# Another order for the units of a pipelined attention round, on one core

## The chip, the core and the metric

The kernel runs on one core of a Trainium2 chip. The metric is the device time of one execution in microseconds (us). Of the kernel before there are three runs: 536.33, 537.93 and 538.74 us, median 537.93. Differences of about 0.5% (2.7 us) are what a measurement of this kernel can tell from no change.

## The reference

Three blocks follow each other. The first is block-causal attention on q, k, v of shape (4, 8, 576, 64), the second a dense layer pair with a bent activation, the third a soft mixture of 8 experts.

```python
scores = scale * np.matmul(q, k.transpose(0, 1, 3, 2))       # masked by blocks of 64
attn = softmax(scores); attn_out = np.matmul(attn, v)
x = attn_out as (2304, 512)
h = x @ w_in                                                  # 512 -> 2048
g = np.where(h >= 1, h, np.where(h <= -1, 0.0, (h + 1) ** 2 / 4))
x2 = g @ w_out
logits = x2 @ phi; slots, expert layers w1 and w2, and the weighted sum back to the tokens
```

## The kernel before, in words

**Engines.** TensorE (PE) multiplies, VectorE (DVE), ScalarE (ACT) and GpSimd (POOL) compute, SyncE (SP) issues all loads in one queue. Each engine works its own list strictly in order, so a list's head that waits holds everything behind it.

**Attention in pairs.** The 4 x 8 heads are worked in 16 pairs of two heads (class `Pair`, numbered 0 to 15, four to a batch; in a tile's name the batch is left out, so `sc_31` is the pair 3 of its batch, part 1). A pair goes through these units; the digit behind a unit's name is its part:

- `lk`, `lq`, `lv`: loads of k, q, v by SP (L60, L73, L74). `kh`, `kl`, `qh`, `ql`: k and q split into a rounded part (ACT; L254, L89) and a rest (POOL L83, DVE L95). After `ql` SP copies a piece of q into a doubled tile `QD` (L99).
- `sc0` to `sc4`: scores on PE (L113, L120), each into one of **two** large PSUM tiles; `mk` adds the mask. `mx` takes row maxima on DVE (L144, L146), `ex` the exponentials on ACT (L151), which frees the score tile for the score part two places later. `rs` sums and inverts on DVE (L157, L158), `no` normalises in place on POOL (L163).
- `pt0` to `pt6`: transposes of the probabilities on PE (L171), each into one of **three** small PSUM tiles of the pool `ptr` (L1131); `pc0` to `pc6` copy them out, `pc1` and `pc3` on DVE (L256), the others on ACT (L254).
- `pa`, `pb`: probabilities times v on PE (L189, L194). `pb` writes its output (`ps..o`) into a `ptr` tile too. `xh`, `xl` take the outputs away: for the first 1024 tokens `xh` is a cast on ACT (L217) and `xl` a subtraction on DVE (L223); for the later ones (pair 8 on, and the end of pairs 4 to 7) `xh` is a copy on DVE (L215) and `xl` does nothing.

**Early work of the second block.** Eleven units of `h = x @ w_in` are worked inside attention (dict `EARLY`, L234). The letters m, x, y, z are four parts of three matmuls on PE (L535) that sum into one `ptr` tile, so that this tile is held for a round and more; `a` is an activation on ACT (L556), `o` two instructions on DVE (L569, L570), the last of which frees the tile. The weights for it come as 64-bit words: `w0` loads a tile `raw` (SP L448), `w1` is one multiplication on ACT (L457) and four bit operations on DVE (L463 to L466), `w2` three operations on POOL (L258, L481, L482).

**What sets the order.** The string `PLAN` (L227) is one round, written out by hand or by a search: `4pt1` means part 1 of `pt` for the pair that started four rounds ago. The function `attention` (L248) unrolls 22 rounds and leaves out what has no pair (L284 to L287). Each engine's list is what the units add to it, one after another; nothing is reordered later. Waits are put in by the framework from who reads and writes what. Once attention is over, `Moe.run` follows with its own order, which is not touched.

```python
plan = [(it - int(u[0]), u[1:]) for it in range(n + 6) for u in PLAN.split()]
```

Of the kernel before, what the change touches and what calls it, by code (L numbers as in the profile page):

```python
# [224 lines left out]


PLAN = """  # L227
6xh1 2ho0 2lq 6xh0 4pt1 4mx0 6xl0 4no4 3sc2 3mx3 3mk2 2kh 4pt2 4ex0 1hy0
4rs1 2kl 4no1 4pt3 4pt5 1hz0 4no0 4pc1 3sc4 3mx2 2w1 6xl1 4pc0 4pt4 5pc6
2w2 3sc1 3ex3 3mk1 4pc2 1w0 5pa 3ex2 4pc5 3rs0 3mx4 3no3 2qh 4pc4 3mx1  # L230
5pb 0lk 2ql 3ex4 3sc0 4pc3 3lv 3mk0 3rs2 2sc3 3no2 2mk3 3pt0 1ha0 0hm0
4pt6 3ex1 0hx0
"""
EARLY = {(9, 0): (0, 0), (10, 0): (0, 1), (11, 0): (0, 2), (12, 0): (0, 3), (13, 0): (1, 0), (14, 0): (0, 4),  # L234
         (15, 0): (1, 1), (16, 0): (0, 5), (17, 0): (1, 2), (18, 0): (0, 6), (19, 0): (1, 3)}
# [980 lines left out]
```

## Time and profile before

| | us |
|---|---|
| median of three runs | 537.93 |
| the profiled execution's own time | 535.42 |
| its span, first to last instruction | 533.6 |
| PE busy | 506.3 (95%) |
| DVE busy | 337.5 (63%) |
| ACT busy | 322.2 (60%) |
| POOL busy | 199.4 (37%) |

The median lies 2.51 us above the profiled execution, and that one 1.82 us above its span. Attention takes the first 206 us of the span, the part from there on belongs to the second and third block. The busy shares above are means over all of it, while the three other engines are far busier in attention than later. A round shows in the trace as the stretch from the start of one pair's `pa` (PE, L189) to the start of the next one's.

### The profile page before, as it was taken

The page shows a single profiled execution, that of the slowest core. Times are in us where ns is not written, and L with a number is a line of the kernel's source. Part 1 is how long each engine was busy: PE and PEld are TensorE (multiplying, and loading weights), DVE is VectorE, ACT ScalarE, POOL GpSimd, SP SyncE. Part 2 cuts the span into 40 slices and gives each one's busy share as a digit, 9 for nine tenths or more (in the row PEclk, how much of TensorE's full clock was granted, in tenths as well). Part 3 has the DMA queues.
Part 4 walks back from the last instruction along what each step waited for, and adds up shares of the span by engine and source line. Part 5 has one row for each costly group of instructions (what it writes and reads, how often), then busy time and mean ns, then how long its engine had stood idle before and what let it go on. Part 6 is the DMA issues. An engine that isn't in the chain of part 4 may idle for free.

```text
span 533.6 us, 11818 instructions
## 1 busy us (share of the span) xinstructions
PE 506.3 (95%) x4538; PEld 382.0 (72%) x4538; DVE 337.5 (63%) x678; ACT 322.2 (60%) x732; POOL 199.4 (37%) x259
## 2 busy tenths in 40 slices
PE   6899999999999999999898999899999999989994
PEld 5688787777777777787666887788767888643463
DVE  7779888788887755888998546824454443531242
ACT  5799998776666644676867888634334545231131
POOL 4889987776665421555542213400001000010000
PEclk9799999999999999999999999999999999999997
DMA  5443453323211136312157874412166496799998
GB/s 177 120 135 114 138 147 85 112 73 112 73 51 50 28 107 211 146 40 80 39 166 217 299 240 166 160 59 79 51 254 226 146 383 208 276 330 390 409 413 313
DMA packets 42711, 91.01 MB, mean 171 GB/s; under 512 B 8736, under 2 KB 18080, under 8 KB 42656
## 3 DMA queue, kind: packets, MB, share of 16 engines
q1 hardware_dynamic: 42656, 90.26, 49.5%
q8 instruction: 36, 0.59, 0.4%
q14 instruction: 19, 0.16, 0.1%
HBM read 74.51 MB, written 14.68 MB: 167 GB/s over the span
## 4 chain that ended last, share of the span: by engine, by line
PE 75%; DVE 8%; ACT 7%; DMA 3%; issue 3%; POOL 2%; SPq 0%; DVEq 0%; ACTq 0%; POOLq 0%
PE h L535 30%; PE sc L120 6%; PE gn L592 5%; PE om L189 4%; PE lt L604 3%; PE s L642 3%; PE eh L998 3%; PE acc L1025 3%; PE ps_1p L171 2%; PE sc L113 2%; PE ps_2p L171 2%; PE ps_3p L171 2%; PE ps_0p L171 2%; ACT pr L151 2%; DMA raw<-in_w_out_dram 2%
## 5 line engine op out<-in xcount | busy, mean ns | idle before, releaser
L535 PE MATMUL h<-xh,w 128*128 128x512 f32 (+1 forms) x384 | 115.6, 369 | 0.0
L535 PE MATMUL h<-xt,w 128*128 128x512 f32 x384 | 98.2, 403 | 0.7 <-DVE g L570 0.2
L163 POOL TENSOR_SCALAR pr<-pr,sm 128x512 f32<-128x512 f32 (+2 forms) x144 | 86.0, 616 | 27.6 <-DVE sm L158 19.8
L151 ACT ACTIVATE pr<-sc,nm 128x512 f32<-128x512 f32 (+2 forms) x144 | 78.9, 561 | 14.6 <-DVE nm L146 8.1
L569 DVE SCALAR_TENSOR_TENSOR g<-g 128x512 f32<-128x512 f32 (+1 forms) x52 | 38.5, 740 | 66.9 <-ACT g L556 66.9
L535 PEld LDWEIGHTS h<-xt,w 128*128 128x128 f32 x384 | 68.3, 188 | 16.4 <-DVE g L570 1.8
L535 PEld LDWEIGHTS h<-xh,w 128*128 128x128 f32 x384 | 69.1, 189 | 13.8 <-issue 3.8
L535 PE MATMUL h<-xl,w 128*128 128x512 f32 (+1 forms) x192 | 68.2, 355 | 0.3 <-POOL xl L409 0.3
L570 DVE TENSOR_TENSOR g<-h,g 128x512 f32<-128x512 f32 (+1 forms) x80 | 50.8, 636 | 14.8 <-ACT g L561 12.8
L146 DVE TENSOR_REDUCE nm<-sc 128x2 f32<-128x1024 f32 (+1 forms) x64 | 51.9, 819 | 10.7 <-PE sc L126 9.6
L556 ACT ACTIVATE g<-h,half 128x512 f32<-128x512 f32 (+1 forms) x52 | 32.4, 623 | 43.3 <-PE h L535 43.0
L673 POOL TENSOR_TENSOR cn<-cn,cm 128x128 f32<-128x128 f32 (+1 forms) x5 | 1.9, 379 | 140.7 <-DVE cm L672 140.7
L120 PE MATMUL sc<-K,Q 64*128 64x512 f32 (+3 forms) x384 | 47.2, 360 | 3.4 <-ACT pr L151 2.9
L254 ACT COPY gn<-gn 128x1024 f32<-128x1024 f32 x35 | 35.3, 1009 | 16.0 <-PE gn L592 15.8
L535 PEld LDWEIGHTS h<-xl,w 128*128 128x128 f32 x192 | 36.4, 189 | 4.5 <-POOL xl L409 0.7
L120 PEld LDWEIGHTS sc<-K,Q 64*128 64x128 f32 x384 | 29.9, 194 | 13.3 <-ACT pr L151 4.7
L474 POOL TENSOR_TENSOR wab<-wab 128x512 f32<-128x512 f32 x16 | 22.0, 1373 | 40.8 <-DVE wab L466 30.7
L481 POOL TENSOR_TENSOR wab<-wab,w 128x256 f32<-128x256 f32 (+1 forms) x23 | 22.7, 985 | 38.9 <-ACT w L254 20.4
L592 PE MATMUL gn<-ident,g 128*128 128x128 f32 x280 | 36.5, 273 | 0.1
L592 PEld LDWEIGHTS gn<-ident,g 128*128 128x128 f32 x280 | 31.9, 140 | 5.3 <-issue 2.5
L464 DVE SCALAR_TENSOR_TENSOR wab<-wab 128x512 uint32<-128x512 uint32 (+1 forms) x39 | 28.5, 730 | 9.9 <-ACT wab L457 6.9
L558 ACT ACTIVATE g<-h,half 128x512 f32<-128x512 f32 x28 | 19.2, 687 | 22.7 <-PE h L535 20.3
(222 smaller groups left out, 896.5 us busy)
## 6 DMA issues: line engine op xcount, KB each, us to landing
ew<-in_w_dram SPq DMA_DIRECT2D x32, 512.0 KB, 5.9
raw<-in_w_in_dram SPq DMA_DIRECT2D x16, 512.0 KB, 5.1
raw<-in_w_out_dram SPq DMA_DIRECT2D x16, 512.0 KB, 4.3
ew<-in_w2a_dram SPq DMA_DIRECT2D x16, 510.0 KB, 8.9
ew<-in_w2b_dram SPq DMA_DIRECT2D x16, 344.0 KB, 6.8
kn<-in_k_dram SPq DMA_DIRECT2D x16, 288.0 KB, 4.4
qn<-in_q_dram SPq DMA_DIRECT2D x16, 288.0 KB, 3.9
vn<-in_v_dram SPq DMA_DIRECT2D x16, 256.0 KB, 3.0
```

The costliest lines, as they stand in the source:

```text
L120: nc.tensor.matmul(sc[:, h, 0:n], self.Q[r, qa, 128 * i:128 * i + 128], self.K[r, ka, 0:n], start=(k == 0), stop=False)
L146: nc.vector.tensor_reduce(out=self.negm[:, 2 * i:2 * i + 2], in_=self.scs[i][:, :, 0:128 * (i + 1)], axis=AX.X, op=ALU.max, negate=True)
L151: self.nc.scalar.activation(pr, sc, AF.Exp, bias=self.negm[:, b:b + 1], accum_out=self.acc[:, b, 0:1])
L163: self.nc.gpsimd.tensor_scalar(out=pr, in0=pr, scalar1=self.sums[:, b:b + 1], scalar2=1.0, op0=ALU.mult, op1=ALU.mult)
L171: nc.tensor.transpose(ps[:, u * P:(u + 1) * P], self.pr[b][:, kc * P:(kc + 1) * P], e.ident)
L254: nc.scalar.copy(dst, src)
L464: v.scalar_tensor_tensor(out=Au, in0=Au, scalar=3, in1=Bu, op0=ALU.logical_shift_left, op1=ALU.bitwise_or)
L535: nc.tensor.matmul(ph[:, 0:n], w[:, wi, kk], self.x(b, kk, xi)[:, 0:n], start=(kk + m == 0), stop=(kk + m == 5))
L556: nc.scalar.activation(g, ph, AF.Relu, bias=e.half[:, 0:1], scale=0.5)
L569: nc.vector.scalar_tensor_tensor(out=g, in0=g, scalar=1.0, in1=g, op0=ALU.min, op1=ALU.mult)
L570: nc.vector.tensor_tensor(out=g, in0=ph, in1=g, op=ALU.max)
L592: nc.tensor.transpose(ps[:, j, i * P:(i + 1) * P], self.gt(b, f)[:, o:o + P], e.ident)
```

## The change

Only the string `PLAN` is replaced. It holds the same units as before, each with the digit that says how many rounds behind it is; most digits grow by one, because the new string is cut at another point of the cycle (it begins just before `pb`, where the old one began just after `hx`). No instruction is added or removed: each engine has as many rows as before.

```diff
 PLAN = """
-6xh1 2ho0 2lq 6xh0 4pt1 4mx0 6xl0 4no4 3sc2 3mx3 3mk2 2kh 4pt2 4ex0 1hy0
...
+4mk1 3qh 6pb 6pa 4mx1 5pc5 2ha0 5pc4 6xh0 3w2 4sc0 2w0 3ql 4ex4 4no3
...
 """
```

Laid over each other as cycles, the two orders differ in these ways. On PE `pb` stands ahead of `pa`, `pt0` moves from behind `sc3` to behind `hy`, and `sc4` moves ahead of `pt5` and `hz`. On ACT the run `kh`, `ex0`, `w1`, `pc0`, `pc6`, `ex3`, `pc2`, `ex2`, `pc5`, `qh`, `pc4`, `ex4`, `a`, `ex1`, `xh1`, `xh0` becomes `kh`, `ex0`, `pc6`, `w1`, `ex3`, `pc2`, `ex2`, `pc0`, `qh`, `pc5`, `a`, `pc4`, `xh0`, `ex4`, `ex1`, `xh1`. On DVE `pc3` moves from behind `ql` to behind `mx2`, and the copies of x are taken apart: the one of `pb`'s output comes first, the ones of `pa`'s output after `mx0`. On SP the loads of q come a round earlier; those of v come later, one round ahead of their `pb` and no longer more than that, and `w0` later too, in the round of its `w1`.

DVE's list in the round in which pair 9 passes `pa` and `pb` (`ps_1o` is `pb`'s output, `om_1` that of `pa`, `nm` are row maxima, `g` and `h` belong to the early unit). Before:

```order
L146 TENSOR_REDUCE nm_3_2056<-sc_31_2118 128x2
L95 SCALAR_TENSOR_TENSOR Q_0_2159<-qn_0_2039,Q_0_2159 128x576
L256 COPY PT_2_2093<-ps_2p_2078 128x512
L157 TENSOR_REDUCE sm_3_2057<-ac_197 128x1
L158 RECIPROCAL sm_3_2057<-sm_3_2057 128x1
L215 COPY xw_148<-om_1_2132 128x128
L215 COPY xw_150<-om_1_2132 128x192
L569 SCALAR_TENSOR_TENSOR g_0_2204<-g_0_2204 128x512
L570 TENSOR_TENSOR g_0_2204<-h_0_2024,g_0_2204 128x512
L215 COPY xw_148<-ps_1o 128x256
L146 TENSOR_REDUCE nm_3_2056<-sc_30_2174 128x2
```

The same stretch of DVE's list now:

```order
L146 TENSOR_REDUCE nm_3_2058<-sc_31_2125 128x2
L215 COPY xw_148<-ps_1o 128x256
L95 SCALAR_TENSOR_TENSOR Q_0_2135<-qn_0_1908,Q_0_2135 128x576
L157 TENSOR_REDUCE sm_3_2059<-ac_197 128x1
L158 RECIPROCAL sm_3_2059<-sm_3_2059 128x1
L569 SCALAR_TENSOR_TENSOR g_0_2163<-g_0_2163 128x512
L570 TENSOR_TENSOR g_0_2163<-h_0_2021,g_0_2163 128x512
L146 TENSOR_REDUCE nm_3_2058<-sc_30_2170 128x2
L215 COPY xw_148<-om_1_2142 128x128
L215 COPY xw_150<-om_1_2142 128x192
```

Between `mx1` (first row) and `mx0` (the `sc_30` row) stood nine instructions and now stand six: `pc3` (the `PT` row) and the two copies from `om_1` are gone from there.

PE's list after the scores `sc3` of the same round (`ps_3p` are transposes `pt0` and `pt1`, `ps_2p` is `pt6`, `h_4` the early unit's parts m and x). Before:

```order
L171 MATMUL ps_3p_2199<-ident,pr_187 128x128
L171 MATMUL ps_3p_2199<-ident,pr_188 128x128
L171 MATMUL ps_3p_2199<-ident,pr_189 128x128
L171 MATMUL ps_3p_2199<-ident,pr_190 128x128
L535 MATMUL h_4_2206<-xt_140,w_1568 128x512 x3
L171 MATMUL ps_2p_2210<-ident,pr_176 128x128
L535 MATMUL h_4_2206<-xt_141,w_1568 128x512 x3
L171 MATMUL ps_3p_2224<-ident,pr_187 128x128
L171 MATMUL ps_3p_2224<-ident,pr_188 128x128
L171 MATMUL ps_3p_2224<-ident,pr_189 128x128
L171 MATMUL ps_3p_2224<-ident,pr_190 128x128
L120 MATMUL sc_02_2231<-K_0_2061,Q_0_2159 128x384 x6
```

The same stretch of PE's list now:

```order
L535 MATMUL h_4_2203<-xt_140,w_1619 128x512 x3
L171 MATMUL ps_2p_2209<-ident,pr_176 128x128
L171 MATMUL ps_3p_2211<-ident,pr_187 128x128
L171 MATMUL ps_3p_2211<-ident,pr_188 128x128
L171 MATMUL ps_3p_2211<-ident,pr_189 128x128
L171 MATMUL ps_3p_2211<-ident,pr_190 128x128
L535 MATMUL h_4_2203<-xt_141,w_1619 128x512 x3
L120 MATMUL sc_02_2230<-K_0_2037,Q_0_2135 128x384 x6
```

`pt0` has left this stretch and `pt1` stands one place earlier, between the two parts of the early unit.

SP's queue at the start (`kn`, `qn` loads of k and q, numbered by pair; `raw` the first weights). Before:

```order
L61 DMA kn_0_205<-in_k_dram 128x576
L61 DMA kn_1_207<-in_k_dram 128x576
L61 DMA qn_0_209<-in_q_dram 128x576
L448 DMA raw_214<-in_w_in_dram 128x1024
L61 DMA kn_2_218<-in_k_dram 128x576
L99 DMA QD_165<-Q_0_216 64x2x64 x2
L61 DMA qn_1_232<-in_q_dram 128x576
```

SP's queue at the start now:

```order
L61 DMA kn_0_205<-in_k_dram 128x576
L61 DMA kn_1_207<-in_k_dram 128x576
L61 DMA qn_0_209<-in_q_dram 128x576
L61 DMA kn_2_213<-in_k_dram 128x576
L61 DMA qn_1_216<-in_q_dram 128x576
L448 DMA raw_220<-in_w_in_dram 128x1024
L99 DMA QD_165<-Q_0_218 64x2x64 x2
```

The first weights have gone from the fourth place to the sixth, behind `kn_2` and `qn_1`.

## Rows read from the trace of the kernel before

**Rows 1.** Windows by round: length, busy of PE, PEld, DVE, ACT, POOL, PEclk, DMA.

```profile
60.80:70.25 9.45, 9.45 (x109) 7.70 (x111) 8.54 (x22) 9.35 (x30) 8.86 (x13) 1.00 0.48 142
70.25:82.48 12.23, 12.23 (x122) 9.85 (x123) 9.67 (x23) 10.29 (x31) 10.14 (x16) 1.00 0.42 123
...
120.25:133.62 13.37, 12.67 (x122) 9.74 (x120) 10.90 (x23) 9.35 (x29) 8.73 (x14) 1.00 0.38 112
...
186.26:196.33 10.07, 9.58 (x92) 7.38 (x93) 5.75 (x14) 4.88 (x16) 3.21 (x7) 1.00 0.43 140
196.33:202.96 6.63, 6.21 (x59) 4.31 (x61) 2.17 (x5) 1.44 (x3) 0.00 (x0) 1.00 0.40 127
```

**Rows 2.** Chain that ended last, 119 to 134.5 us: start, length, what.

```profile
120.92 1.18 DVE Q L95
122.11 0.60 DVE PT L256
...
122.97 0.45 DVE xw L215 x2
123.42 1.03 DVE g L569
...
124.48 0.70 DVE g L570
...
127.05 0.48 ACT PT L254
...
127.58 0.66 PE ps_2p L171 x4
```

**Rows 3.** PE's timeline, same round: start, length, instruction, [idle before <-who].

```profile
127.58 0.66 PE L171 MATMUL ps_2p<-ident,pr 128*128 128x128 f32 x4 [0.58 <-ACT PT L254]
```

**Rows 4.** Chain that ended last, PE in the round from 70.25 us.

```profile
70.25 1.66 PE om L189 x16
...
73.68 0.78 PE sc L120 x6
...
75.09 0.69 PE h L535 x3
```

**Rows 5.** ACT's timeline in a round without early work, from 51.33 us.

```profile
54.75 0.67 ACT L254 CAST K<-kn 128x576 fp32r<-128x576 f32 x1
...
56.98 0.72 ACT L151 ACTIVATE pr<-sc,nm 128x512 f32<-128x512 f32 x1
```

**Rows 6.** Chain that ended last, the start.

```profile
8.45 2.58 ACT pr L151 x8
...
15.63 1.90 PE ps_0p L171 x8
```

**Rows 7.** ACT's timeline at the start.

```profile
7.79 0.43 ACT L457 ACTIVATE wab<-raw 128x256 f32<-128x256 f32 x1 [1.47 <-DMA raw<-in_w_in_dram]
```

**Rows 8.** Windows at the start, columns as in rows 1.

```profile
3.00:4.00 1.00, 1.00 (x12) 1.00 (x11) 0.87 (x8) 0.00 (x0) 0.00 (x0) 1.00 1.04 396
...
12.00:18.00 6.00, 5.01 (x28) 3.95 (x30) 4.09 (x10) 4.75 (x16) 6.00 (x9) 0.50 0.35 73
...
19.00:25.00 6.00, 4.31 (x44) 3.73 (x42) 5.50 (x14) 5.59 (x16) 4.24 (x6) 1.00 0.38 142
...
29.00:32.00 3.00, 3.00 (x30) 2.83 (x28) 2.68 (x8) 2.30 (x7) 1.55 (x4) 1.00 0.33 126
```

**Rows 9.** Chain that ended last, the end of attention and what follows.

```profile
205.20 0.65 PE ps_3o L189 x8
205.85 52.85 PE h L535 x228
```

**Rows 10.** The page, part 5: busy us, mean ns of one | idle before.

```profile
L163 POOL TENSOR_SCALAR pr<-pr,sm 128x512 f32<-128x512 f32 (+2 forms) x144 | 86.0, 616 | 27.6 <-DVE sm L158 19.8
...
L569 DVE SCALAR_TENSOR_TENSOR g<-g 128x512 f32<-128x512 f32 (+1 forms) x52 | 38.5, 740 | 66.9 <-ACT g L556 66.9
```

**Rows 11.** The page, part 6: DMA issues, KB each, us to landing.

```profile
vn<-in_v_dram SPq DMA_DIRECT2D x16, 256.0 KB, 3.0
```

More of the change, by code (lines that the diff above doesn't have):

```diff
@@ L227 @@
 PLAN = """
-6xh1 2ho0 2lq 6xh0 4pt1 4mx0 6xl0 4no4 3sc2 3mx3 3mk2 2kh 4pt2 4ex0 1hy0
[L229 to L232, printed above, removed]
+4mk1 3qh 6pb 6pa 4mx1 5pc5 2ha0 5pc4 6xh0 3w2 4sc0 2w0 3ql 4ex4 4no3
+4rs2 4mk0 3sc3 4no2 3mk3 4no4 4ex1 1hm0 2ho0 5pt6 4pt1 4mx0 6xh1 2kh 6xl0
+0lk 5lv 4ex0 1hx0 3sc2 5pc6 3mk2 3mx3 4pt2 4pt3 4pc1 4rs1 2kl 3mx2 1hy0
+4pc3 2w1 6xl1 3ex3 1lq 4pc2 4no1 3ex2 3rs0 4no0 4pt0 3sc4 4pt5 1hz0 4pt4
+3mx4 3sc1 4pc0
 """
```

## The prediction

> **What bounds the kernel now.** I began with the windows by round, since the change touches attention alone. A round without early work takes 9.45 us, and PE is busy for all of it; the first one with four parts of an early unit takes 12.23 us, and PE is busy for all of that too [rows 1]. So 9.45 and 12.23 us are what PE's own work costs, and what a round takes beyond them is waiting. From pair 8 on a round takes 13.37 us with the same parts in it [rows 1]: over 1.1 us of waiting in each of them.
>
> Then the chain shows where. In such a round it runs on DVE and not on PE: `ql` 1.18 us, the copy `pc3` 0.60, two copies of x 0.45, the early unit's two instructions 1.03 and 0.70, in all 120.92 to 125.18; behind that ACT works off `ex0`, `w1` and the copy `pc0`, and PE gets on with `pt1` at 127.58 [rows 2]. PE's timeline has the same instruction with 0.58 us of idle time ahead of it, ended by ACT's copy [rows 3]; the rest of the waiting is spread ahead of the early unit, whose tile the 0.70 us instruction frees. What holds PE is a chain of three engines through the three small PSUM tiles, though none of them is full: DVE is busy for 10.90 and ACT for 9.35 of 13.37 us [rows 1].
>
> **The change part by part.** No instruction goes or comes, so every term is waiting. All are sums against the profiled execution: its span 533.6 us, 535.42 us with what lies around it, 2.51 us under the median shown.
>
> *Rounds with early work.* Two things go. `pt0` no longer stands ahead of `pt1`, so `pt1` needs no `pc0`; and DVE reaches the instruction that frees the early unit's tile without `pc3` and the two copies of x from `pa` (0.60 and 0.45 us [rows 2]) ahead of it. What is late next: `pt1` now takes the tile which that instruction frees, and ahead of it on DVE stands the copy of `pb`'s output, which waits for `pb`. I lay the two side by side from the start of `pb`. DVE: `pb` 0.65 us [rows 9], a copy at most 0.45, `ql` 1.18, the two small ones of `rs` 0.26 (from 122.71 to 122.97), 1.03 and 0.70 [rows 2]: 4.27 us. PE: `pa`, `pb` and `sc0` 3.43 (70.25 to 73.68), `sc3` 0.78 and the first early part 0.69 [rows 4]: 4.90 us; the 0.63 us that are missing up to 75.09 are mostly `pt0`, which has left. DVE is there 0.63 us early. It needs `ex4` done by then for `rs`; ACT has 13.37 less 9.35 us of idle time to place [rows 1], and `qh`, `pc5`, `a` and `pc4` ahead of `ex4` all work on results of the round before. In rounds whose x is cast on ACT `pt1` waits for the subtraction `xl0` instead, behind `mx0`; `ql` then starts without waiting for `pb`, so about as much is left. `pc3` now stands behind `mx2` and ahead of `w1`: its cover is DVE's slack, 12.23 less 10.90, and if that were gone `mx4` and `mx1` would be late by up to 0.60 us. So the waits go if the side by side holds. Their size: from 82.48 to 186.26 us (ends of [rows 1]) eight rounds take 103.78 us against 8 x 12.23 = 97.84, that is 5.94 us. Bounds: nothing and 5.9 us gained. I take 5.0, nearer the upper end, since each hand-over keeps some of its time.
>
> *Last two rounds.* 10.07 and 6.63 us with PE busy 9.58 and 6.21 [rows 1], so 0.91 us of waiting, of the same kind. Between 0 and 0.9; I take 0.4.
>
> *Rounds without early work.* ACT is busy 9.35 of 9.45 us [rows 1], so its order matters to a tenth. Before, it came from `kh` to `ex3` in 2.23 us (54.75 to 56.98) with `pc0` among them [rows 5]. `pc0` leaves that run, which brings `ex3` forward, but `xh0` and `xh1` now wait for `pb` and `pa`, and `kh` still for `sc0`. There are four such rounds, the last of them the 9.45 us one. Nothing lost, or up to 0.5 us in each; I take 0.1 each, a loss of 0.4.
>
> *SP.* The load of v goes from over a round ahead of `pb` to under one. It takes 3.0 us to land [rows 11], and the queue reaches it after `ql` and two short copies, in the first half of a 9.45 us round, so the rest of the round hides it; without that cover `pb` would start late by what is missing. Loads of q come earlier and cost nothing.
>
> *The start.* The first weights go from fourth to sixth in SP's queue, behind two loads of 128 x 576 words, 295 KB each. ACT's multiplication of them already waits for them, 1.47 us, until 7.79 [rows 7], and `ex3` of the first pair stands right behind it on ACT. At 396 GB/s [rows 8] the two loads cost 1.49 us: the multiplication starts at 9.28, and with its 0.43 us `ex3` starts at 9.71 against 8.45 [rows 6], 1.3 us later. `sc4`, `ex2` and `ex4` follow it. Against that `pt0` and `pt1` stood together on the chain in front of `sc2`, 1.90 us [rows 6], and half of that, 0.95, leaves it in each of the two rounds before the first `pa`. Sum 1.3 - 1.9 = -0.6. PE's clock is the unsafe part: it was granted 0.50, the level of 1.2 GHz, from 12 to 18 us, after PE had waited for ACT, and 1.00 from 19 us, after it had worked through [rows 8]. A longer wait can move both edges. Between 1.9 us gained and 2.5 lost; I take 0.5 gained.
>
> Sum: -5.0 - 0.4 + 0.4 - 0.5 = -5.5 us. Span 528.1, the execution 529.9, and from the median **532.4 us**.
>
> **The rivals.**
>
> *DVE is held by GpSimd.* The early unit's first instruction takes 740 ns on average [rows 10] and 1.03 in the round above, `ql` 1.18 [rows 2]; both read two SBUF operands while GpSimd normalises or splits k. In the new order they stand closer together, in the time in which GpSimd works off `no3`, `no2` and `no4` without a break. If each loses another 0.62 us, the mean length of one normalisation [rows 10], the 0.63 us in hand becomes 0.61 us of waiting in each of the ten rounds from 70.25 to 196.33, 6.1 us against the 5.5 of the sum: 538.5. Against it: both already stand in their long form in the sum. The Trainium skill states this as a rule (SBUF — State Buffer, section SBUF: two separate sides): a VectorE instruction with two SBUF inputs and a GpSimd instruction lock the port pair for each other, and the loser waits for the whole of the other's instruction. The 1.03 against 740 ns agrees with it; by the rule a whole normalisation would be added each time.
>
> *The gain is taken back after attention.* PE works 52.85 us without a break from 205.85 us [rows 9], and only then waits for weights. If these came by a clock of their own, that wait would grow by what attention gained: 537.9. Against it, their loads stand behind attention's last loads in SP's one queue and would move with them.
>
> *The start stays on the slow clock.* If the later `ex3` cuts PE's work up so that 1.00 is not granted before the first `pa`, the 4.31 us of busy time from 19 to 25 and the 3.00 us from 29 to 32 [rows 8] are doubled: 7.3 and the 1.3 us give 8.6, against 5.0 and 0.4 gained and 0.4 lost in the rounds: 3.6 us slower, 541.5. It decides at the stretch that lay from 12 to 18 us: if PE is busy there for less than the 5.01 of 6.00 us before. For it, ACT already waits for this very load; against it, `pt0` and `pt1` still fill PE there.
>
> **How the numbers follow.** Forecast 0.64, GpSimd 0.14, taken back 0.08, slow start 0.14. The forecast's own range is from -5.9 - 0.9 - 1.9 = -8.7 (529.2) to about -2.5 (535.4), all faster by over 0.5% (2.7 us, about what can be told from no change) but for its last edge. The GpSimd case reaches, with less than a whole normalisation added, into the faster side with 0.02 of its 0.14, and 0.12 lies within. That makes 0.66 faster, 0.20 the same, 0.14 slower. The range takes in the two cases of no change and leaves out the slow start and a little at either end: 529.0 to 538.4.
>
> **What would show it.** Right: rounds of pairs 5 to 12 at 12.2 to 12.5 us; no idle time of PE ended by ACT's copy ahead of `pt1`; rounds without early work at 9.45 to 9.6; the first `pa` at 31 to 32.5 us; `pa` of pair 15 by 198 us. Wrong: `pt1` waiting for the early unit's second instruction or for `xl0` (DVE too late); `sc2` or `sc4` waiting for ACT in the short rounds; ACT idle for the first weights until after 9.3 us and a granted clock of 0.50 beyond 19 us; or an early end of attention, and a longer wait for weights near 260 us.

## The result and the profile after

The changed kernel takes 531.06 us in the median of four runs (528.83 to 532.08), the kernel before 537.13 beside it (four runs). The ratio is 0.9901, with a 95% interval of 0.9875 to 0.9928: by it 5.3 us less (the two medians lie 6.1 apart). The profiled execution after took 532.08 us, the longest of its four, with a span of 530.2 against 533.6 us. Forecast were 532.4 us and a gain of 5.5; the sum came out, but two of its terms, the last two rounds and the start, did not.

The windows by round of the changed kernel (columns as in [rows 1]): the last round without early work, the first with it, the one with PE's work of the 13.37 us round, and the two last.

```profile
64.24:73.88 9.64, 9.64 (x111) 7.85 (x107) 8.56 (x22) 9.30 (x30) 8.86 (x14) 1.00 0.52 154
73.88:86.15 12.27, 12.27 (x124) 9.87 (x120) 9.96 (x26) 10.92 (x32) 9.80 (x15) 1.00 0.44 122
122.93:135.19 12.26, 12.26 (x124) 9.87 (x120) 10.38 (x23) 9.70 (x28) 9.18 (x14) 1.00 0.42 122
184.23:193.37 9.14, 9.14 (x94) 7.56 (x90) 5.14 (x13) 4.87 (x16) 3.14 (x6) 1.00 0.51 149
193.37:199.32 5.95, 5.95 (x59) 4.49 (x58) 2.27 (x5) 1.10 (x3) 0.00 (x0) 1.00 0.36 114
```

PE is busy for the whole of every one of them. All nine rounds with early work take 12.26 us, and the 13.37 us of [rows 1] are gone. The last two take 9.14 and 5.95 us in place of 10.07 and 6.63. The short rounds take 9.64 in place of 9.45.

PE's timeline in such a round, the place of [rows 3]:

```profile
127.17 0.96 PE L535 MATMUL h<-xt,w 128*128 128x512 f32 x3
127.97 0.27 PE L171 MATMUL ps_1p<-ident,pr 128*128 128x128 f32 x1
128.07 0.60 PE L171 MATMUL ps_2p<-ident,pr 128*128 128x128 f32 x4
```

No idle time stands ahead of `pt1` (128.07) or ahead of the early part. VectorE's timeline of the same round, the place of [rows 2]:

```profile
124.19 0.95 DVE L95 SCALAR_TENSOR_TENSOR Q<-qn,Q 128x576 fp32r<-128x576 f32 x1
...
125.31 0.81 DVE L569 SCALAR_TENSOR_TENSOR g<-g 128x512 f32<-128x512 f32 x1
126.16 0.69 DVE L570 TENSOR_TENSOR g<-h,g 128x512 f32<-128x512 f32 x1
...
127.10 0.54 DVE L215 COPY xw<-om 128x128 f32<-128x128 f32 x2
...
131.20 0.69 DVE L256 COPY PT<-ps_2p 128x512 f32<-128x512 f32 x1
```

From the start of `pb` at 122.93 the early unit's second instruction is done after 3.92 us (126.16 + 0.69), and `pt1` starts after 5.14. VectorE has 1.2 us in hand. The copies of x (127.10) and `pc3` (131.20) come later. The chain of waits through these rounds holds PE's instructions alone.

The start went the other way. Its windows in the changed kernel, against [rows 8]:

```profile
10.00:20.00 10.00, 8.10 (x44) 6.11 (x45) 7.08 (x18) 7.37 (x25) 7.39 (x10) 0.51 0.46 130
20.00:27.00 7.00, 5.23 (x51) 4.42 (x49) 5.70 (x14) 6.68 (x22) 5.69 (x10) 0.98 0.21 75
27.00:33.50 6.50, 6.45 (x32) 5.42 (x31) 4.60 (x9) 4.69 (x15) 4.46 (x9) 0.50 0.52 143
```

The granted clock was 0.51 from 10 to 20 us and 0.50 from 27 to 33.5, some 17 us at the level of 1.2 GHz with the edges; before it was about 10 (11.75 to 18.5 and 25.4 to 28.8). The first `pb` starts at 35.34 us, the first `pa` before at 32.29. PE's two long waits near these falls:

```profile
11.04 1.78 PE L113 MATMUL sc<-K,QD 128*128 128x288 f32 x6 [2.21 <-DVE wab L464]
...
25.04 0.55 PE L120 MATMUL sc<-K,Q 64*128 64x128 f32 x6 [1.46 <-ACT pr L151]
```

It waited 2.21 us for the buffer of `sc3`, up to 11.04, and 1.46 us for ScalarE, up to 25.04. The first fall came inside the first wait, between 9.5 and 9.75 us, the second at 26.7, 1.7 us after the second wait had ended. `sc4` then took 1.78 us. Attention's last product ends where PE's early block goes on without a break, as in [rows 9]:

```profile
199.39 0.80 PE ps_3o L189 x8
...
202.28 3.86 PE h L535 x16
```

From the last `pb` or `pa` to the end of the span there are 330.9 us, against 330.7 before. Nothing was taken back there.

In the two profiles the 3.4 us of span are, start of round to start of round: nine rounds with early work 116.01 to 110.35, -5.66; the last two -1.61; four short rounds 37.89 to 38.54, +0.65; the start +3.05; the rest +0.17.

### The profile page after: what moved, and what is told of

It is laid out like the page before. It is cut to its first block, busy times and chain, and to the rows that moved or that the text cites. A ratio compares the mean times of both kernels' runs of the same rounds, so it can differ in the third digit from the quotient of the medians.

```text
span 530.2 us, 11838 instructions
## 1 busy us (share of the span) xinstructions
PE 506.9 (96%) x4538; PEld 386.1 (73%) x4538; DVE 335.5 (63%) x678; ACT 324.4 (61%) x732; POOL 202.0 (38%) x259
## 4 chain that ended last, share of the span: by engine, by line
PE 82%; DVE 5%; DMA 4%; ACT 4%; issue 2%; POOL 1%; SPq 0%; ACTq 0%; DVEq 0%; POOLq 0%
PE h L535 32%; PE sc L120 7%; PE gn L592 5%; PE om L189 5%; PE lt L604 4%; PE s L642 3%; PE eh L998 3%; PE sc L113 3%; PE ps_1p L171 3%; PE ps_2p L171 2%; PE ps_3p L171 2%; PE ps_0p L171 2%; PE acc L1025 2%; PE om L194 2%; DVE wab L464 1%
## 5 line engine op out<-in xcount | busy, mean ns | idle before, releaser
L535 PE MATMUL h<-xt,w 128*128 128x512 f32 x384 | 99.4, 403 | 0.0
L163 POOL TENSOR_SCALAR pr<-pr,sm 128x512 f32<-128x512 f32 (+2 forms) x144 | 88.5, 632 | 25.3 <-DVE sm L158 23.6
L569 DVE SCALAR_TENSOR_TENSOR g<-g 128x512 f32<-128x512 f32 (+1 forms) x52 | 36.9, 710 | 66.9 <-ACT g L556 66.3
```

Of the source, the lines that this page charges most:

```text
L163: self.nc.gpsimd.tensor_scalar(out=pr, in0=pr, scalar1=self.sums[:, b:b + 1], scalar2=1.0, op0=ALU.mult, op1=ALU.mult)
L535: nc.tensor.matmul(ph[:, 0:n], w[:, wi, kk], self.x(b, kk, xi)[:, 0:n], start=(kk + m == 0), stop=(kk + m == 5))
L569: nc.vector.scalar_tensor_tensor(out=g, in0=g, scalar=1.0, in1=g, op0=ALU.min, op1=ALU.mult)
```

## Experiments on the rounds

The question is which of the moved units gave the 5.7 and 1.6 us. My theory had two parts: `pt0` ahead of `pt1`, and VectorE's row ahead of the instruction that frees a small tile.

**Undo pt0.** From the changed kernel:

```diff
-... 3sc3 4no2 3mk3 4no4 ... 4ex0 1hx0 ... 4no0 4pt0 3sc4 ... 3sc1 4pc0
+... 3sc3 4no2 3mk3 4pt0 4no4 ... 4ex0 4pc0 1hx0 ... 4no0 3sc4 ... 3sc1
```

> The changed kernel with one thing undone: pt0 stands behind sc3 and ahead of pt1 again, and its copy pc0 behind ex0 on ScalarE. If pt0 ahead of pt1 made the rounds of 13.4 us (pt1 then needs a small tile that ScalarE's late copy frees), the rounds of pairs 8 to 12 go from 12.26 back to 13.0 to 13.4 us, with idle time of PE ahead of pt1 ended by a PT copy on ACT, and the time goes up by 5 to 8 us to 536 to 539. If VectorE's row (pc3 and the copies of x ahead of the early unit's second instruction) made them, the rounds stay at 12.3 to 12.5 us and the time within 1.5 us of 531.

Measured: 533.95 us, ratio to the kernel before 0.996 (0.9938 to 0.9981). The rounds with early work take 12.38 us: the first half of my theory falls for them. In them the chain is PE's alone, so 0.12 us is what PE's own order costs. The short rounds rise to 9.93 us, the last two take 9.82 and 5.95. The chain in a short round:

```profile
71.33 0.64 ACT PT L254 x2
...
71.97 0.45 ACT wab L457
72.42 1.34 ACT pr L151 x4
...
73.81 1.06 PE sc L113 x6
```

`pc0` and `pc6` (the two copies), `w1` and `ex3` follow each other on ScalarE, and `sc4` waits for `ex3`. By this chain, taking `pc0` out of ScalarE's run is what the move of `pt0` bought in the short rounds.

**Undo pc3.**

```diff
-... 2w0 3ql 4ex4 ... 1hy0 4pc3 2w1 ...
+... 2w0 3ql 5pc3 4ex4 ... 1hy0 2w1 ...
```

> The changed kernel with another thing undone: the copy pc3 stands behind ql of the next round on VectorE again, so that it holds its small tile through pa and pb; pt0 stays where the change put it. If VectorE's row was what the long rounds paid, those of pairs 8 to 12 go from 12.26 to 12.8 to 13.4 us and the time up by 3 to 7 us to 534 to 538. If only pt0 mattered, they stay at 12.3 to 12.5 us and the time within 1.5 us of 531.

Measured: 541.15 us, ratio 1.0088 (1.0054 to 1.0123), slower than before. Rounds with early work 12.87, short ones 10.51, the last two 11.05 and 5.95. The chain ahead of a `pb`:

```profile
138.53 0.69 ACT g L556
...
139.23 0.60 ACT PT L254
...
139.87 0.65 PE ps_1o L189 x3
```

`pb` waits for ScalarE's activation `a` and the copy behind it: with `pc3` behind `ql` its small tile is still held when `pb` asks for one, so that `pb` has to take the tile that this copy frees. Here `pc3` costs through the tile that it holds, and not through its 0.60 us on VectorE. My prediction had only the latter.

**Put the copies of x back.**

```diff
-... 1hm0 2ho0 5pt6 4pt1 4mx0 6xh1 2kh ...
+... 1hm0 6xh1 2ho0 5pt6 4pt1 4mx0 2kh ...
```

> The changed kernel with the copies of x from pa's output back ahead of the early unit's instructions on VectorE (xh1 ahead of ho0); all else as changed. If each instruction ahead of the early unit's second one on VectorE costs a round its own length, the rounds whose x is copied by VectorE (pairs 8 to 12) take 12.26 + 0.45 = 12.7 us, those of pairs 4 to 7, whose x is cast on ScalarE, 12.26 to 12.4, and the time goes up by 1.5 to 2.5 us to 532.5 to 533.5. If VectorE has slack there once pc3 is gone, all rounds stay at 12.26 to 12.35 us and the time within 0.7 us of 531.

Measured: 534.68 us, 0.9973 (0.9944 to 1.0002). The other way round: pairs 8 to 12 stay at 12.26 us, the copies of 0.54 us fit into what VectorE has in hand. But the rounds of pairs 5 to 7 take 13.05, 12.91 and 12.91 us, and the round of pair 13 10.12 in place of 9.14. The chain in pair 5's:

```profile
89.31 0.33 ACT xt L217
...
89.66 0.29 DVE xw L215
89.95 0.72 DVE g L569
...
90.70 0.69 DVE g L570
91.39 0.33 DVE nm L146
91.72 0.34 DVE xt L223
...
92.19 0.63 PE ps_3p L171 x4
```

In these rounds `pb`'s small tile is freed by the subtraction `xl0` (91.72), which stands behind the early unit and `mx0` on VectorE; `pt1` takes that tile and waits 0.42 us for it. From pair 8 on a copy ahead of `ql` frees it. The early unit itself is later too, since one output of `pa` is partly cast by ScalarE (`xt`) and partly copied by VectorE (`xw`), and the copy starts only when the cast is done, 0.38 us after `pa`'s end at 89.28. The prediction had treated these rounds as ScalarE's, with about as much in hand. The two read different columns of one bank of `om`. The Trainium skill (PSUM — Partial Sum Buffer, section PSUM bank collisions raise a hardware error) says that two engines cannot access one bank within the same partition at the same time; the trace agrees as far as one comes after the other here.

**VectorE's row alone, pt0 as well, and pc3 alone,** all from the kernel before:

```diff
 dve_moved
-6xh1 2ho0 2lq 6xh0 4pt1 4mx0 6xl0 ... 3mx2 2w1 ... 3sc0 4pc3 3lv
+2ho0 2lq 6xh0 4pt1 4mx0 6xh1 6xl0 ... 3mx2 4pc3 2w1 ... 3sc0 3lv
 both_moved: the same, and
-... 4pc1 3sc4 ... 6xl1 4pc0 4pt4 ... 3ex2 4pc5 ... 2mk3 3pt0 1ha0
+... 4pc1 4pt0 3sc4 ... 6xl1 4pt4 ... 3ex2 4pc0 4pc5 ... 2mk3 1ha0
 pc3_moved
-... 3mx2 2w1 ... 3sc0 4pc3 3lv
+... 3mx2 4pc3 2w1 ... 3sc0 3lv
```

> The kernel before with only VectorE's row changed: pc3 behind mx2 and xh1 behind mx0; pt0 stays ahead of pt1 and pc0 where it was. If VectorE's row is the gain (0.60 + 0.45 us a round), the rounds of pairs 8 to 12 take 12.4 to 12.6 us in place of 13.4, about as with pt0 moved as well (12.44), and the rounds without early work show whether pc3 (10.0 to 10.1 us, as with both) or pt0 (9.5) lengthened them. If pt0 ahead of pt1 matters, the rounds of pairs 8 to 12 stay at 12.8 to 13.3 us with PE idle ahead of pt1.

> The kernel before with three units moved and nothing else: pt0 and its copy pc0 to where the changed kernel has them, pc3 behind mx2, and the copy xh1 behind mx0; pa still comes ahead of pb, and all loads stand as in the kernel before. If these moves are the gain, the rounds of pairs 8 to 12 take 12.3 to 12.6 us in place of 13.4, and as the start keeps its loads, the first pa comes by 32 to 33 us and the time is 527 to 531, below the changed kernel's 531. If the place of pb ahead of pa, or the other shifts, are needed too, the rounds stay above 12.8 us and the time at 533 to 537.

> The kernel before with one unit moved: the copy pc3 from behind ql to behind mx2 on VectorE. With the copies of x moved too, the rounds of pairs 8 to 12 went from 13.4 to 12.24 us. If pc3's 0.60 us and the 0.45 us of the copies each count in full, they now take 12.7 to 12.8 us. If the copies of x stand in slack once pc3 is gone (as they did when put back into the changed kernel, where these rounds stayed at 12.26), they take 12.2 to 12.35 us and pc3 alone is the gain in the rounds; those without early work should take 10.0 to 10.1 us, as with both moved.

| start of `pa` to start of `pa`, us | first `pa`/`pb` at | short rounds | pair 4 | pairs 5 to 7 | pairs 8 to 12 | last two | median | ratio to before |
|---|---|---|---|---|---|---|---|---|
| before | 32.29 | 9.47 | 12.23 | 12.46 to 12.68 | 12.67 to 13.42 | 10.06, 6.63 | 537.13 | 1 |
| pc3_moved | 37.37 | 10.08 | 12.24 | 13.17 | 12.38 to 13.05 | 10.07, 6.63 | 539.78 | 1.009 (1.0068 to 1.0113) |
| dve_moved | 35.28 | 10.08 to 10.36 | 12.23 | 12.24 | 12.24 to 12.39 | 9.12, 5.97 | 533.73 | 0.9972 (0.9946 to 0.9999) |
| both_moved | 35.72 | 10.07 | 12.45 | 12.44 | 12.45 | 10.09, 5.99 | 535.86 | 0.9991 (0.9961 to 1.0022) |
| after | 35.34 | 9.64 | 12.27 | 12.26 | 12.26 | 9.14, 5.95 | 531.06 | 0.9901 (0.9875 to 0.9928) |

Two moves on VectorE, `pc3` and `xh1`, give all that the change gives in the rounds of pairs 5 to 14. `pc3` alone makes the rounds of pairs 5 to 7 longer. Its chain in pair 5's:

```profile
92.97 0.22 ACT xt L217
...
93.21 0.29 DVE xw L215
93.50 0.77 DVE g L569
...
96.22 0.32 ACT wab L457
96.54 0.49 ACT PT L254
...
97.07 0.66 PE ps_3p L171 x4
```

The cast and the copy of x put the early unit late, `mx0` and `ex0` follow, then `w1` and `pc0` on ScalarE, and `pt1` waits for that copy, as it did in [rows 2]. With both moves that wait is gone, though `pt0` still stands ahead of `pt1`. Neither 12.7 to 12.8 nor 12.2 to 12.35 came for pairs 8 to 12 as a whole: `pc3` alone gives a small part there, 12.38 to 13.05 us, and `xh1` on top of it the rest. The two don't simply add, since `pc3` alone makes the rounds of pairs 5 to 7 longer (13.17 us), and with `xh1` they take 12.24. `xh1` without `pc3` was not run from the kernel before; in the changed order the rounds are long without the move of `pc3` (12.87 us in pc3_back), with `xh1` moved. Moving `pt0` as well brings nothing in the old order, it costs 0.2 us a round. But the two moves cost the short rounds 0.6 us each. VectorE's and PE's timelines there, in `dve_moved`:

```profile
73.09 0.69 DVE L256 COPY PT<-ps_1p 128x512 f32<-128x512 f32 x1
...
75.29 0.54 DVE L223 TENSOR_TENSOR xt<-om,xt 128x256 fp32r<-128x256 f32 x2
```

```profile
75.89 0.44 PE L189 MATMUL om<-PT,vn 128*64 128x256 f32 x2 [0.36 <-DVE xt L223]
```

`pc3` (73.09) now stands ahead of the bit operations and of the subtractions `xl1` (75.29), which free `om`; `pa` needs that bank first thing in the round and waits 0.36 us for them. That is the loss that I had named for the case without cover, but for other instructions (`mx4` and `mx1`). The changed kernel puts `pb` ahead of `pa`, so that `om` is asked for 0.80 us later, and it pays only 0.17 a round. 0.3 us are `pt0`'s, by the run that undoes it. That `pb` ahead of `pa` covers `pc3` is read from these traces; it was not run by itself. Nor was `pt0` moved without `pc3`. PE is busy throughout in the changed kernel's short rounds, so its 0.17 us there is PE's own; which pairs of neighbours cost it stays open.

The last two rounds are the move of `xh1`: pc3_moved leaves them at 10.07 and 6.63 us, and dve_moved, which differs from it by `xh1` alone, takes 9.12 and 5.97. In the kernel before the copies of `pa`'s output wait for the end of `pa`, the early unit's two instructions stand behind them, and PE waits for the second (the round of pair 14):

```profile
200.55 0.33 PE L171 MATMUL ps_3p<-ident,pr 128*128 128x128 f32 x1 [0.42 <-DVE g L570]
```

The round of pair 13 is long again in three runs, and PE's timelines show a wait in each, for the same instruction in x_back and for one of ScalarE's copies in pt0_back and both_moved:

```profile
191.51 0.63 PE L171 MATMUL ps_3p<-ident,pr 128*128 128x128 f32 x4 [0.54 <-DVE g L570]
```

```profile
193.05 0.66 PE L171 MATMUL ps_3p<-ident,pr 128*128 128x128 f32 x4 [0.51 <-ACT PT L254]
```

```profile
197.53 0.63 PE L171 MATMUL ps_3p<-ident,pr 128*128 128x128 f32 x4 [0.77 <-ACT PT L254]
```

So `pt0` ahead of `pt1` does bring the forecast wait for `pc0` in this one round of pt0_back, though not in the nine with early work.

## Experiments on the start

**The first weights.** The first 9 units in another order (`FILL`, empty before):

```diff
-... 0lq 0kh 2lk 0kl 1lq 0qh 1w0 ...
+... 0lq 1w0 0kh 2lk 0kl 1lq 0qh ...
```

> The changed kernel with only the load of the first weights put back into fourth place of SyncE's queue, as in the kernel before. If the late load makes the loss of 3.05 us in the start, ScalarE multiplies the first weights at 7.8 to 8.2 us in place of 9.17, ex3 starts at 8.4 to 8.7 in place of 9.51, and the first pb comes at 32.5 to 34.3 us in place of 35.34: 1 to 3 us off the time. If it is rather the first q, which landed at 6.08 in place of 5.05 us, or the clock alone, ex3 starts at 9.4 to 9.6, the first pb at 34.8 to 35.6, and the time stays within 0.7 us of 531.

Measured: 531.77 us, 0.9927 (0.989 to 0.9965), first `pb` at 35.37: no gain. ScalarE's timeline in this run:

```profile
6.04 0.68 ACT L89 ACTIVATE Q<-qn 128x576 fp32r<-128x576 f32 x1 [4.02 <-DMA qn<-in_q_dram]
...
8.19 0.44 ACT L457 ACTIVATE wab<-raw 128x256 f32<-128x256 f32 x1 [0.91 <-DMA raw<-in_w_in_dram]
9.41 0.69 ACT L151 ACTIVATE pr<-sc,nm 128x512 f32<-128x512 f32 x1 [0.78 <-DVE nm L146]
```

The multiplication starts 0.98 us earlier than with the change, at 8.19. But `ex3` then waits 0.78 us for VectorE's maxima, and these hang on the first q, which ScalarE gets at 6.04 us here, at 6.11 in the profile after and at 5.07 before. From q to `ex3` there are 3.38 us before ([rows 6]) and 3.37 here. So in the profiled run after, q alone put `ex3` at 9.49, and the late weights 0.02 us behind that. The granted clock is 0.50 from 10 to 20 and from 27 to 33.5 us here too.

The three loads ahead are the same in every kernel. Over the fourteen traces of this study q's split starts between 5.07 and 6.85 us, with no order to it: 5.53 to 6.85 in the other kernels that load as before, 5.11 to 6.49 in those that load as after. The profile before was the earliest of all, and a part of the +3.05 us is that. It was also the one with the shortest slow stretch: the start was at 0.50 for about 10 us there, and for 14 to 20 in the eight other traces whose waits are not filled, pc3_moved and dve_moved among them, which keep the old loads and PE's old order.

**The clock.** Matmuls of zeros fill PE's waits:

```diff
+    e.idle = e.ppv.tile([P, 512], F32, tag="pv", name="idle")
+IDLE = {(0, "sc4"): 16, (0, "sc0"): 6, (1, "sc0"): 11}          # idle_fill
+IDLE = {(0, "sc4"): 32, (0, "sc0"): 12, (1, "sc3"): 5, (1, "sc0"): 20, (2, "sc3"): 5}   # idle_full, idle_before
     for i, u in fill + plan[len(fill):]:
+        for _ in range(IDLE.get((i, u), 0)):
+            nc.tensor.matmul(e.idle[:, 0:P], e.zero, e.zero, start=True, stop=True)
```

> The changed kernel with 33 extra matmuls of zeros (128x128, into a PSUM bank that is free until the first pa, results not used): 16 ahead of sc4 and 6 ahead of sc0 of the first pair, 11 ahead of sc0 of the second, in the three places where PE waited 2.21, 0.70 and 1.46 us for ScalarE. If the start's loss is the clock, which fell to 0.50 at 9.9 and at 27 us, each time soon after such a wait, for about 16 us in all against 10 in the kernel before, it is granted 1.00 for most of the first 35 us, and the first pb comes at 31 to 33.5 us in place of 35.34: 2 to 4 us off the time, 527 to 529. If ScalarE's and GpSimd's chain sets the start whatever the clock, the first pb stays at 34.5 to 36 us and the time within 1 us of 531.

> The same with 66 extra matmuls of zeros, ahead of eleven score and transpose units of the first three pairs, since at full clock PE will wait at more places than the trace shows. If the clock is the loss, 1.00 holds through the first 35 us and the first pb comes at 30 to 33 us, the time at 526 to 529. If the extra matmuls themselves get into the path (33 more at 0.13 us each is 4.3 us), the first pb comes later than with 33 of them by up to 4 us. If the chain of ScalarE and GpSimd sets the start, the first pb comes at 34.5 to 36 us again.

> The changed kernel with the same 74 extra matmuls of zeros. With 33 of them the clock still fell once, at 24 us, behind a wait that they did not fill; with more ahead of sc4 and of the second sc0 it should stay at 1.00 to the first pb, which comes at 30 to 31.3 us (31.27 with 33 of them): 526 to 527.5 us. Against idle_before this gives the change at full clock: 8 rounds 5.9 and the last two 1.6 us gained, four short rounds 0.65 lost, 5 to 7.5 us if the starts are then alike. If the start is longer by the change's order itself, the difference is under 5 us.

> The kernel before with 74 extra matmuls of zeros ahead of five score units of the start (32 ahead of sc4, 12 ahead of sc0 of pair 0 and 5 ahead of sc3 of pair 1, then 20 and 5 one pair later), results not used; the order is that of the kernel before. If the clock costs this kernel's start about 5 us too (10 us at 0.50), the first pa comes at 28 to 30.5 us in place of 32.29 and the time falls by 2 to 4 us to 531.5 to 533.5. If its start is set by ScalarE and GpSimd, it stays within 1 us of the kernel before.

| | first `pa`/`pb` at | median | ratio to before |
|---|---|---|---|
| idle_fill | 31.27 | 527.61 | 0.985 (0.9814 to 0.9886) |
| idle_more | 31.53 | 527.12 | 0.9839 (0.9802 to 0.9876) |
| idle_full | 30.64 | 526.95 | 0.9845 (0.9825 to 0.9864) |
| idle_before | 30.06 | 532.73 | 0.9961 (0.994 to 0.9983) |

The windows of idle_full, to be laid beside those of the changed kernel:

```profile
10.00:20.00 10.00, 8.44 (x80) 6.88 (x81) 7.74 (x19) 8.71 (x29) 8.88 (x13) 1.00 0.45 146
20.00:27.00 7.00, 6.15 (x70) 4.67 (x69) 5.78 (x14) 6.45 (x20) 6.46 (x10) 1.00 0.22 54
27.00:33.50 6.50, 6.50 (x78) 5.64 (x78) 5.78 (x15) 6.46 (x20) 5.95 (x10) 1.00 0.43 134
```

The clock stays at 1.00, the level of 2.4 GHz, through the whole start. PE's timeline of the same run:

```profile
7.78 1.96 PE L293 MATMUL idle<-warm 128*128 128x128 bf16 x32
11.05 1.04 PE L114 MATMUL sc<-K,QD 128*128 128x288 f32 x6 [1.31 <-POOL w L260]
```

`sc4` starts at 11.05 us here and at 11.04 in the changed kernel, so the two starts are alike up to there. It takes 1.04 us in place of 1.78, and the first `pb` comes at 30.64 in place of 35.34: the 4.70 us in between are the clock's. With 33 matmuls (idle_fill) PE still waited 1.11 us behind the last of them, and the clock fell once more; a window of idle_fill:

```profile
24.00:27.00 3.00, 3.00 (x17) 2.08 (x15) 1.79 (x2) 1.94 (x8) 3.00 (x5) 0.50 0.59 141
```

idle_more, with another set of places, lost it once as well, from 11.5 to 14.8 us, behind a wait of 1.71 us that ended at 11.21. The Trainium skill (TensorE: Matmul & The Clock Gate, section HAM oscillation — how this bites in real kernels) says of a kernel that waits for DMA between groups of matmuls that such a wait makes the engine's clock fall and the next group start slowly. These runs agree, with waits for ScalarE: in idle_full and idle_before, where they were filled further, neither fall came.

From `sc4` to the first product with v, idle_full takes 30.64 - 11.05 = 19.59 us and idle_before, whose `sc4` starts at 10.45, 19.61. At full clock the two orders of the start are equal. In the profiles they took 24.30 after and 22.30 before (32.29 - 9.99). So of the +3.05 us, 1.05 lie ahead of `sc4`, where q came 1.04 later, and 2.00 behind it, and those are the clock's. That the change's order brought them is not shown: dve_moved and pc3_moved, with the old order on PE, took 23.12 and 25.68 us for the same stretch, and raw_fourth, x_back, pt0_back and pc3_back, with the new one but for their own edit, 22.89 to 25.52. By the ratios to the kernel before, filling the waits took 3.0 us off the changed kernel (0.9901 to 0.9845) and 2.1 off the kernel before (0.9961). That leaves about 0.9 us for the order, which these intervals cannot tell from nothing. The late weights do show in idle_full: q is there at 5.11, `ex3` could start at 8.49, and starts at 9.52, right behind the multiplication. They cost up to 1.0 us where q comes early and nothing where it comes late.

**Both orders joined.** The units of the kernel before up to the first round with early work, by `FILL`, then the changed order, with the matmuls of idle_full.

> A kernel meant to beat both: the units run in the order of the kernel before up to the first round with early work, and in the changed order from there on (the same units, each once), with the same 74 extra matmuls of zeros. If the two orders' gains add, the start is that of idle_before, the rounds without early work take 9.47 us in place of 9.63 (0.6 us less in four), and the later ones 12.26: 524.5 to 527, up to 1.5 us below idle_full. If the seam between the orders costs a wait, the round at the seam is over 13 us and the time is 527 to 529.

Measured: 527.24 us, 0.9855 (0.9828 to 0.9882), not to be told from idle_full. Three short rounds take 9.45 to 9.49 us, as hoped; the seam costs 0.4, and q came at 6.84 in the profiled run, and its start was 31.83. A window of that start and one of the round at the seam:

```profile
9.25:12.50 3.25, 3.25 (x33) 2.98 (x30) 3.08 (x6) 2.28 (x7) 0.95 (x3) 0.50 0.53 136
...
60.22:70.13 9.91, 9.53 (x112) 7.71 (x108) 9.01 (x23) 9.83 (x31) 9.23 (x15) 1.00 0.35 114
```

The clock fell to 0.50 here with the same 74 matmuls in place, while PE was at work: it had waited 1.72 us for ScalarE's q ahead of the first scores, up to 7.58, and that wait is not filled. So the filling held the clock where q came at 5.11 and 5.53 us (idle_full, idle_before) and did not where it came at 6.84.

idle_full has the lowest median of the kernels that beat both, 526.95 us, by its ratio 1.55% under the kernel before; idle_fill, with 33 matmuls in three places, cannot be told from it.

## Why the prediction was right, and where it was not

- *Rounds with early work: -5.0 forecast, -5.66 measured.* Right in mechanism for VectorE's row, and at the upper bound: nothing was left of the hand-overs for which I had kept 0.9 us. Wrong in its first reason: `pt1` waiting for `pc0` was the end of a chain that VectorE made late. With VectorE's row in order, `pt0` ahead of `pt1` costs 0.12 us in these rounds (pt0_back) and brings no wait there. The chain of [rows 2] had shown this: ScalarE's pieces stand in it behind the 0.70 us instruction. The side by side held: 0.63 us in hand was worked out, 1.2 measured: VectorE's side took 3.92 us for the 4.27 of the sum, as `ql` and the early unit's first instruction became shorter (0.95 and 0.81 for 1.18 and 1.03, or 1.11 in the same kind of view), and PE's took 5.14 for 4.90. That `pc3` also holds one of three tiles past `pb` was missing from it.
- *Last two rounds: -0.4 forecast, -1.61 measured,* beyond my bound of 0.9. I had taken PE's busy time for its own cost, 9.58 and 6.21 us; the changed kernel needs 9.14 and 5.95. The move of the copies gives it (dve_moved: 9.12 and 5.97, pc3_moved 10.07 and 6.63): they had made the early unit wait for `pa`. The term was of the right kind and set too small.
- *Short rounds: +0.4 forecast, +0.65 measured.* The size was near, but not the cause: I expected ScalarE, and PE is busy for all of the time. That every term is waiting was wrong here, since PE's own work takes longer in another order.
- *Start: -0.5 forecast, +3.05 measured in the profiles,* outside my bounds of -1.9 and +2.5. This step failed. The gain of 2 x 0.95 us for `pt0` is not seen: at full clock the orders are equal. The 1.3 us for the weights came to 1.0 at most, and only where q came early. The clock, which I had called the unsafe part and given no term of its own, made 2.00 us of the profiled pair's difference, and the arrival of q the other 1.05. How much of either belongs to the change stays open; by the filled runs it is about 0.9 us, or nothing. The slow-start rival was right about its place, and its size was too large, since 1.00 was granted in between.
- *Why the sum held.* In part by luck, as misses of opposite sign met. The rounds with early work and the last two gained 1.9 us more than forecast, the short rounds lost 0.25 more, and the profiled start went 3.55 the wrong way. By the ratio the gain is 5.3; with -5.66, -1.61 and +0.65 in the rounds that leaves about 1.3 us for an average start, less than the profiled pair's 3.05, and it fits that the profile before had the earliest q and the profile after was the longest of its runs. This last step is worked out, not measured in a trace. idle_full against idle_before, at full clock in both, gives 5.8 us by the medians.
- *GpSimd holding VectorE* fell: both instructions came out shorter, and no wait was added. *Gain taken back after attention* fell: 330.7 and 330.9 us.

## What to carry to other kernels

When a wait ends at an engine's instruction, follow the chain further back before naming what to move: here ScalarE's copy stood at its end, and VectorE's place for two copies was the cause. Count the small tiles that a late copy holds as well as the time that it takes. And price a change to the start at either level of PE's clock: a wait of 1 to 2 us there cost more by the slow matmuls behind it than by itself, and matmuls of zeros in the waits took that back (3.0 us by the ratios 0.9901 and 0.9845, 4.1 by the medians), where the first q came early. One profile of a start is not enough to price it: the arrival of the third load alone moves it by up to 1.78 us.

## What the runs showed of the hardware

- One level of the clock against the other, in the same instruction: six matmuls of `sc4` 1.78 us at 0.50 and 1.04 at 1.00. Of 74 extra matmuls the 32 ahead of `sc4` (1.96 us) took no time from the work behind them, as 1.31 us of the wait were left; behind the two groups of five no wait was left, so that these may have cost a little.
- Three loads of the same size at the head of one queue: the third was there between 5.07 and 6.85 us in fourteen traces, a spread of 1.78 us.
- Two engines that read different columns of one PSUM bank go one after the other in this program (x_back): VectorE's copy of 0.29 us waited for ScalarE's cast of 0.32 and started 0.03 us after it had ended.
